# Replanned costs, a shared port that is counted fairly, and a weight-splitting step that may run on VectorE or ScalarE

## The chip, the cores and the metric

The kernel runs on one core of a Trainium2 chip. The metric is the device time of one execution in microseconds (us). The engines are TensorE (PE in the profile, PEld for its weight loads), VectorE (DVE), ScalarE (ACT), GpSimd (POOL) and SyncE (SP), which here issues all DMAs.

## What is computed

A chunked linear attention over 4 sequences of 768 tokens and 8 heads, and behind it two feed-forward layers of width 2048 on the 3072 tokens, with ELU and with Mish:

```python
# per chunk c of each sequence and head, cum = cumsum(log a):
M = einsum('bhin,bhjn->bhij', Cc, Bc) * exp(cum_i - cum_j) * causal
y = einsum('bhij,bhjd->bhid', M, xc) + einsum('bhin,bhnd->bhid', Cc, state) * exp(cum)
state = exp(sum(la)) * state + sum_j(Bc_j * xc_j * exp(cum_last - cum_j))
...
h = x @ w_in;  g = where(h > 0, h, exp(min(h, 0)) - 1);   x = g @ w_out      # layer 1
h = x @ w_in;  g = h * tanh(log1p(exp(min(h, 20))));      y = g @ w_out      # layer 2
```

The weights arrive in double precision, 64 bits each. Precision is kept by splitting each operand into a high and a low part and summing three products.

## The kernel before

The 3072 tokens go through the layers in seven blocks of 384, 384, 512, 512, 512, 512 and 256 columns, and each block of a layer in 16 slots, one for each 128 of the 2048 hidden units. A slot s is: six matmuls into a tile `h` (lines 769 to 771, `emit_h(s)`), the activation into `w` (ELU: `elu_1` on ScalarE line 785, `elu_2` on ScalarE line 791 or VectorE line 793, `elu_3` on VectorE lines 799 and 801; Mish: `mish_1`, ScalarE line 816), the split into `gh` (`split_hi`, lines 356 and 358) and `gl` (`split_lo`, line 812, GpSimd or VectorE), and the second product into `acc`. Slots 0 to 15 are layer 1 of block 0, 16 to 31 layer 1 of block 1, 32 to 47 layer 2 of block 0, and so on; h(s) stands below for the six matmuls of slot s. There are two `h` tiles in this phase, so h(s) waits until the activation has read h(s-2).

The attention runs in 32 tiles of 96 tokens, woven in between: a DMA brings the row `d`, `at_diff` adds to it (line 543, two halves, each on GpSimd or VectorE), `at_mask` masks it (GpSimd, line 547), `at_exp` takes the exponential (ScalarE, line 552), the scores are multiplied in (`at_p0`, line 654, or `at_p`, line 666, VectorE), and TensorE forms `ys` (line 697).

The weights come in 32 jobs of 256 by 256 double-precision numbers. A job has five steps. `job_1` takes the top three bits of each low word (VectorE, line 332, in place in the tile `raw`); `job_2` scales the high words (ScalarE, line 341, function Prelu); `job_3` joins both (VectorE, line 348); `job_4` makes the high part (line 356 on ScalarE or 358 on VectorE) and `job_5` the low part (line 372, GpSimd or VectorE).

Nothing in this order is written by hand. Every piece is a `step` with an engine (or several to choose from, `alt`), a cost in us, and its dependences. `run_steps` simulates the five engines by these costs: it takes the engine that can start soonest, on it the ready step with the least latest start `late`, and for a step with a choice the engine on which `end` is least. VectorE steps in the set `lock` are not started while a GpSimd step runs, nor the other way (`held`), since both use one port. ScalarE keeps one table of functions at a time: the planner charges LOAD, 1.4 us, for a switch between the tables of `exp` (also that of `job_2`) and of `mish`. What the plan gives is the order in which the instructions stand on each engine; on the chip each engine works through its own list and waits at the head of it.

Of the kernel before, what the change touches and what calls it, by code (L numbers as in the profile page):

```python
# [10 lines left out]
I32 = mybir.dt.int32  # L11
AF = mybir.ActivationFunctionType
# [5 lines left out]
def tile_chain(  # L18
# [54 lines left out]
    LOAD, HOLD = 1.4, 6.0  # L73

# [45 lines left out]
    def run_steps():  # L120
# [208 lines left out]
    def job_1(j):  # L329

        lw = raw[j][:, :, :, 0]
        nc.vector.tensor_scalar(  # L332
# [609 lines left out]
    for j, (key, k) in enumerate(jobs):  # L942
# [11 lines left out]
        q1 = step((V, 0.36, lambda j=j: job_1(j)), q0)  # L954
# [3 lines left out]
        q3 = step((V, 0.65, lambda j=j: job_3(j)), q1, q2)  # L958
# [28 lines left out]
    def out_of_y(i, y):  # L987

        YHI[i], YLO[i] = {}, {}
        for q in pieces(i):  # L990
            w = q[3] / T
            YHI[i][q[0]] = step((A, 0.11 + 0.1 * w, lambda q=q: at_y_hi(i, *q)), y, xy_f["x", q[0]][1])
            YLO[i][q[0]] = step((V, 0.07 + 0.2 * w, lambda q=q: at_y_lo(i, *q)), YHI[i][q[0]])
        return list(YHI[i].values()) + list(YLO[i].values())

    def three_parts(i, need):
# [3 lines left out]
        a1 = step((A, 0.82, lambda: at_split_1(i)), need, sn)  # L1000
        a2 = step(alt(lambda e: at_split_2(i, e), (V, 0.40), (G, 0.45)), a1, rn)
        a3 = step((A, 0.62, lambda: at_split_3(i)), a2)
        a4 = step(alt(lambda e: at_split_4(i, e), (V, 0.40), (G, 0.45)), a3)
# [7 lines left out]
    def two_scores(i, a5, tf, ex, r_n, cold):  # L1011
        pz = []
        for z in range(2):
            pf, pn = take("s")
            sc = step((PE, 0.4 if cold else 0.33, lambda z=z: at_scores(i, z)), a5, pn)
# [77 lines left out]
    for i in range(NB, tiles):  # L1093
# [26 lines left out]
        rc2 = step(alt(lambda e, i=i: at_rc2(i, e), (V, 0.27), (A, 0.41)), rc)  # L1120
# [33 lines left out]
    for s in range(len(order) * NF):  # L1154
# [11 lines left out]
        pe = 6 * (0.0115 + n / 2370)  # L1166
# [10 lines left out]
        ca, cv, ct, cg = 0.10 + n * 0.00071, 0.07 + n * 0.00052, 0.07 + n * 0.00104, 0.08 + n * 0.00243  # L1177
# [84 lines left out]
```

## Time and profile before

| | |
|---|---|
| median of three runs | 630.92 us (628.60 to 631.34) |
| the profiled execution | 628.61 us |
| its span, first to last instruction | 626.7 us |
| TensorE busy | 606.7 us (97%) |
| VectorE / ScalarE / GpSimd busy | 453.0 / 367.9 / 193.8 us |
| chain that ended last | PE 82%, DVE 10%, ACT 4%, issue 2% |

The span is shorter than the profiled execution by 1.9 us, which lie around it. TensorE's busy time includes the pipelined tails of matmuls, so its idle time, not its busy time, says where it waits. The chain that ended last is followed back from the last instruction: an engine with no share of it had its work hidden.

### The profile page before, as it was taken

The page shows a single profiled execution, that of the slowest core. Times are in us where ns is not written, and L with a number is a line of the kernel's source. Part 1 is how long each engine was busy: PE and PEld are TensorE (multiplying, and loading weights), DVE is VectorE, ACT ScalarE, POOL GpSimd, SP SyncE. Part 2 cuts the span into 40 slices and gives each one's busy share as a digit, 9 for nine tenths or more (in the row PEclk, how much of TensorE's full clock was granted, in tenths as well). Part 3 has the DMA queues.
Part 4 walks back from the last instruction along what each step waited for, and adds up shares of the span by engine and source line. Part 5 has one row for each costly group of instructions (what it writes and reads, how often), then busy time and mean ns, then how long its engine had stood idle before and what let it go on. Part 6 is the DMA issues. An engine that isn't in the chain of part 4 may idle for free.

```text
span 626.7 us, 10880 instructions
## 1 busy us (share of the span) xinstructions
PE 606.7 (97%) x3876; PEld 513.3 (82%) x3876; DVE 453.0 (72%) x885; ACT 367.9 (59%) x681; POOL 193.8 (31%) x243
## 2 busy tenths in 40 slices
PE   6899999899999999999999999999999999999996
PEld 5776789798988778888888888888888888988895
DVE  5989799998878888764768765878765445844453
ACT  4678887558776677543786645878644313542121
POOL 4456844255366466000454201435300000000000
PEclk9799999999999999999999999999999999999999
DMA  7889592013656545000545201444200001100010
GB/s 155 214 247 313 162 325 44 24 20 71 121 93 87 119 104 85 3 1 8 104 91 91 44 1 44 88 93 74 60 0 1 0 5 25 33 1 1 1 35 17
DMA packets 133653, 47.07 MB, mean 75 GB/s; under 512 B 116672, under 2 KB 122432, under 8 KB 133600
## 3 DMA queue, kind: packets, MB, share of 16 engines
q1 hardware_dynamic: 133600, 46.39, 33.1%
q8 instruction: 30, 0.49, 0.3%
q14 instruction: 23, 0.19, 0.1%
HBM read 32.31 MB, written 3.24 MB: 57 GB/s over the span
## 4 chain that ended last, share of the span: by engine, by line
PE 82%; DVE 10%; ACT 4%; issue 2%; DMA 1%; POOL 0%; DVEq 0%; ACTq 0%
PE acc L863 14%; PE h L769 13%; PE h L770 12%; PE h L771 12%; PE acc L864 7%; PE acc L832 5%; PE acc L833 5%; PE acc L834 5%; PE ys L697 2%; PE ys L727 2%; DVE raw L348 1%; PE s L660 1%; DVE raw L332 1%; PE acc L837 1%; DVE gl L812 1%
## 5 line engine op out<-in xcount | busy, mean ns | idle before, releaser
L769 PE MATMUL h<-xyh,wi 128*128 128x512 f32 (+2 forms) x448 | 167.2, 373 | 6.4 <-ACT w L816 3.7
L770 PE MATMUL h<-xyl,wi 128*128 128x512 f32 (+2 forms) x448 | 161.5, 361 | 0.0
L771 PE MATMUL h<-xyh,wi 128*128 128x512 f32 (+2 forms) x448 | 161.1, 360 | 0.0
L863 PE MATMUL acc<-wo,gh 128*128 128x512 f32 x384 | 142.3, 403 | 0.0
L812 DVE TENSOR_TENSOR gl<-w,gh 128x512 fp32r<-128x512 f32 (+2 forms) x187 | 124.2, 666 | 20.9 <-ACT gh L356 11.7
L816 ACT ACTIVATE w<-h 128x512 f32<-128x512 f32 (+2 forms) x112 | 59.5, 536 | 109.4 <-PE h L771 66.7
L864 PE MATMUL acc<-wo,gl 128*128 128x256 f32 x384 | 107.6, 280 | 0.0
L769 PEld LDWEIGHTS h<-xyh,wi 128*128 128x128 f32 x448 | 84.5, 189 | 23.1 <-ACT w L816 5.3
L358 DVE CAST gh<-w 128x512 fp32r<-128x512 f32 (+2 forms) x112 | 46.9, 420 | 69.2 <-PE acc L863 48.2
L771 PEld LDWEIGHTS h<-xyh,wi 128*128 128x128 f32 x448 | 84.5, 189 | 10.7
L770 PEld LDWEIGHTS h<-xyl,wi 128*128 128x128 f32 x448 | 84.7, 189 | 9.1 <-DVE xyl L714 0.5
L863 PEld LDWEIGHTS acc<-wo,gh 128*128 128x128 f32 x384 | 72.2, 188 | 15.4
L785 ACT ACTIVATE w<-h 128x512 f32<-128x512 f32 (+2 forms) x96 | 51.8, 542 | 52.5 <-PE h L771 35.0
L356 ACT ACTIVATE gh<-w 128x512 fp32r<-128x512 f32 (+2 forms) x96 | 55.3, 578 | 32.5 <-PE acc L833 23.3
L864 PEld LDWEIGHTS acc<-wo,gl 128*128 128x128 f32 x384 | 72.5, 189 | 1.7
L832 PE MATMUL acc<-gh,wo 128*128 128x512 f32 (+2 forms) x192 | 70.4, 366 | 0.9 <-DVE xyl L848 0.9
L812 POOL TENSOR_TENSOR gl<-w,gh 128x512 fp32r<-128x512 f32 (+2 forms) x21 | 26.1, 1242 | 142.0 <-ACT gh L356 112.5
L833 PE MATMUL acc<-gh,wo 128*128 128x512 f32 (+2 forms) x192 | 69.6, 363 | 0.0
L834 PE MATMUL acc<-gl,wo 128*128 128x512 f32 (+2 forms) x192 | 69.6, 363 | 0.0
L793 DVE TENSOR_SCALAR w<-w 128x512 f32<-128x512 f32 (+2 forms) x78 | 37.0, 476 | 36.5 <-ACT w L785 35.9
L801 DVE TENSOR_TENSOR w<-h,w 128x512 f32<-128x512 f32 (+2 forms) x78 | 48.8, 628 | 2.1
L543 POOL TENSOR_TENSOR d<-d,dk 96x384 f32<-96x384 f32 x36 | 34.4, 966 | 28.1 <-DMA d<-cum_d 20.5
(100 smaller groups left out, 848.4 us busy)
## 6 DMA issues: line engine op xcount, KB each, us to landing
d<-cum_d SPq DMA_DIRECT2D x31, 288.0 KB, 3.6
raw<-in_moe_w_in_dram SPq DMA_DIRECT2D x16, 512.0 KB, 6.0
raw<-in_moe_w_out_dram SPq DMA_DIRECT2D x16, 512.0 KB, 6.0
xs<-in_x_dram SPq DMA_DIRECT2D x32, 96.0 KB, 2.8
bc<-in_C_dram SPq DMA_DIRECT2D x32, 48.0 KB, 2.7
bc<-in_B_dram SPq DMA_DIRECT2D x32, 48.0 KB, 2.7
out_dram<-o SPq DMA_DIRECT2D x16, 96.0 KB, 1.9
bc<-bc SPq DMA_DIRECT2D x84, 16.0 KB, 1.9
```

The lines of the kernel that those rows point to most:

```text
L356: nc.scalar.activation(out=out, in_=in_, func=AF.Copy)
L769: nc.tensor.matmul(out=h, lhsT=hi[:, k, fs], rhs=xh[:, k, :], start=(k == 0), stop=False)
L770: nc.tensor.matmul(out=h, lhsT=hi[:, k, fs], rhs=xl[:, k, :], start=False, stop=False)
L771: nc.tensor.matmul(out=h, lhsT=lo[:, k, fs], rhs=xh[:, k, :], start=False, stop=(k == 1))
L785: nc.scalar.activation(out=new_w(s), in_=st[s][0], func=AF.Exp)
L812: alu(eng).tensor_tensor(out=gl, in0=w, in1=gh.bitcast(F32), op=ALU.subtract)
L816: nc.scalar.activation(out=new_w(s), in_=st[s][0], func=AF.Mish)
L832: nc.tensor.matmul(out=y, lhsT=hi[:, f % FP, ds], rhs=gh, start=(f == 0), stop=False)
L833: nc.tensor.matmul(out=y, lhsT=lo[:, f % FP, ds], rhs=gh, start=False, stop=False)
L834: nc.tensor.matmul(out=y, lhsT=hi[:, f % FP, ds], rhs=gl, start=False, stop=(f == NF - 1))
L863: nc.tensor.matmul(out=y, lhsT=gh[:, ts], rhs=w[:, :, f % FP, :], start=(f == 0), stop=False)
L864: nc.tensor.matmul(out=y[:, 0], lhsT=gl[:, ts], rhs=w[:, 0, f % FP, :], start=False, stop=(f == NF - 1))
```

## The change

All in the planner's numbers and rules, and one step with a second form:

- `job_1` may now run on ScalarE as well, there as a Copy of the low word, read as an unsigned integer, times 7.4999 / 2^32 and written as an integer; the planner chooses (VectorE 0.36, ScalarE 0.57). ScalarE gets 23 of the 32 jobs, VectorE keeps 9.
- In the comparison of engines (`end`), a choice between GpSimd and VectorE now counts the time for which the other one holds the port.
- A VectorE step that needs the port is held back when a GpSimd step that has no other engine is ready and more urgent by over YIELD, 2.0 us.
- Some twenty costs are new (below, a part of them).

```diff
-            r = max(free[e], ready(k, e))
+            r = max(free[e], ready(k, e), held[V] if e == G else held[G] if e == V and k in lock else 0.0)
...
+            wait_g = [(k, r) for k, o, r, _ in open_[G] if len(steps[k][0]) == 1 and free[G] <= free[V]]
...
                     if e == V and k in lock:
                         r = max(r, held[G])
+                        if any(late[q] + YIELD < late[k] and q2 <= max(r, free[V]) for q, q2 in wait_g if q != k):
+                            continue
...
-    def job_1(j):
+    def job_1(j, eng):
...
+        if eng == A:
+            nc.scalar.activation(out=lw, in_=lw.bitcast(U32), func=AF.Copy, scale=7.4999 * 2.0**-32)
+            return
...
-        q1 = step((V, 0.36, lambda j=j: job_1(j)), q0)
+        q1 = step(alt(lambda e, j=j: job_1(j, e), (V, 0.36), (A, 0.57)), q0)
...
-        q5 = step(alt(lambda e, j=j: job_5(j, e), (G, 1.33), (V, 0.60)), q4,
+        q5 = step(alt(lambda e, j=j: job_5(j, e), (G, 1.33), (V, 0.65)), q4,
...
-        a2 = step(alt(lambda e: at_split_2(i, e), (V, 0.40), (G, 0.45)), a1, rn)
+        a2 = step(alt(lambda e: at_split_2(i, e), (V, 0.50), (G, 0.50)), a1, rn)
...
-        ca, cv, ct, cg = 0.10 + n * 0.00071, 0.07 + n * 0.00052, 0.07 + n * 0.00104, 0.08 + n * 0.00243
+        ca, cv, ct, cg = 0.12 + n * 0.00080, 0.09 + n * 0.00058, 0.09 + n * 0.00110, 0.10 + n * 0.00243
```

Two places show what the new plan does to the lists of the engines.

VectorE at the start, from the first difference of tile 1 on (L543 is `at_diff`, L654 `at_p0`, L714 the low part of a tile's output), before:

```order
L543 TENSOR_TENSOR d<-d,dk 96x384
L654 TENSOR_TENSOR r<-s,d 96x192 x4
L543 TENSOR_TENSOR d<-d,dk 96x384
L358 COPY f32t<-p_tr 112x384
L654 TENSOR_TENSOR r<-s,d 96x192 x4
L543 TENSOR_TENSOR d<-d,dk 96x384
```

The same place of the changed kernel, whose lines are ten further down:

```order
L553 TENSOR_TENSOR d<-d,dk 96x384 x3
L664 TENSOR_TENSOR r<-s,d 96x192 x4
L553 TENSOR_TENSOR d<-d,dk 96x384 x2
L664 TENSOR_TENSOR r<-s,d 96x192 x4
L553 TENSOR_TENSOR d<-d,dk 96x384
L664 TENSOR_TENSOR r<-s,d 96x192 x4
```

All six differences of the tiles 1 to 3 now stand on VectorE, three of them ahead of the first `at_p0`; three stood on GpSimd.

ScalarE where the first Mish slots begin (L816 is `mish_1`, L356 the high parts `wi`, `wo` of weights and `gh`, L844 the high part of layer 1's result), before:

```order
L356 ACTIVATE wo_1433<-raw_1046 128x512
L816 ACT_TABLE_LOAD
L816 ACTIVATE w<-h 128x384
L356 ACTIVATE gh<-w 128x384
L356 ACTIVATE wi_1465<-raw_1061 128x512
L356 ACTIVATE wo_1491<-raw_1072 128x512
L816 ACTIVATE w<-h 128x384 x4
L844 ACTIVATE xyh<-acc 128x384
```

There in the changed kernel (L826 is `mish_1`, L340 `job_1` on ScalarE, L351 `job_2`, L534 a step of the attention):

```order
L826 ACT_TABLE_LOAD
L826 ACTIVATE w<-h 128x384 x2
L534 ACTIVATE stk<-r_1463 96x16x16
L534 ACTIVATE stk<-r_1465 96x8x32
L340 ACTIVATE raw_1178<-raw_1178 128x512
L351 ACT_TABLE_LOAD
L351 ACTIVATE raw_1178<-raw_1178 128x512
L826 ACT_TABLE_LOAD
L826 ACTIVATE w<-h 128x384 x2
L854 ACTIVATE xyh<-acc 128x384
```

The high parts of the weights that stood between the first two Mish steps have gone elsewhere, and a `job_2` now stands between Mish steps with a table load on both sides. Over slots 32 to 47 there was one such pair of loads (for an `at_exp`); there are five now, three for a `job_2` and two for an `at_exp`.

Counted by stages, in the order in which the plan issues its steps: between h(0) and h(48) VectorE has 29 `job_1` before and 7 now; ScalarE gets 10 between h(0) and h(16), 8 up to h(32) and 4 up to h(48). VectorE has there 5 `at_diff`, 4 `split_lo`, 2 `job_5` and 2 `job_4` more than before. After h(48) no `job_1` was left before, and none is now; VectorE has 4 `at_diff` and 4 `at_split_4` more there and 9 `split_lo` and 10 `elu_2` fewer.

## Rows read from the trace of the kernel before

**Rows 1.** Stretches from h(0), h(16), h(32), h(48) on: span, PE, PEld, DVE, ACT, POOL, PEclk.

```profile
0.00:23.00 23.00, 17.31 (x193) 14.32 (x193) 15.14 (x46) 11.61 (x23) 9.51 (x19) 0.81 0.76 167
23.00:71.30 48.30, 45.22 (x339) 34.30 (x337) 43.59 (x83) 39.32 (x78) 30.77 (x32) 0.99 0.94 269
71.30:108.40 37.10, 35.41 (x184) 32.07 (x183) 33.27 (x55) 28.16 (x59) 19.49 (x20) 1.00 0.56 162
108.40:148.70 40.30, 36.63 (x234) 33.39 (x233) 39.19 (x70) 24.46 (x46) 18.49 (x20) 1.00 0.13 25
148.70:621.30 472.60, 472.06 (x2936) 399.20 (x2934) 321.06 (x631) 263.86 (x479) 115.59 (x155) 1.00 0.26 49
```

**Rows 2.** TensorE in order of time: start, duration, instruction, in brackets the idle time before.

```profile
28.48 0.41 PE L769 MATMUL h<-xyh,wi 128*128 128x384 f32 x1 [1.45 <-ACT g L791]
39.28 0.92 PE L837 MATMUL acc<-g,raw 128*128 128x384 f32 x2 [0.81 <-DVE raw L348]
...
115.52 0.44 PE L769 MATMUL h<-xyh,wi 128*128 128x384 f32 x1 [1.73 <-ACT w L816]
119.39 0.45 PE L769 MATMUL h<-xyh,wi 128*128 128x384 f32 x1 [1.09 <-ACT w L816]
147.58 0.45 PE L769 MATMUL h<-xyh,wi 128*128 128x384 f32 x1 [0.85 <-ACT w L816]
```

**Rows 3.** Single lines: count, ns shortest/median/longest, first and last start, tile shapes.

```profile
L332 DVE TENSOR_SCALAR raw<-raw x32: 411/423/1249, 17.7 to 131.6; 128x512 int32<-128x512 int32 x32
...
L543 POOL TENSOR_TENSOR d<-d,dk x36: 827/840/1334, 10.3 to 437.6; 96x384 f32<-96x384 f32 x36
L543 DVE TENSOR_TENSOR d<-d,dk x26: 542/555/1665, 11.4 to 437.3; 96x384 f32<-96x384 f32 x26
```

**Rows 4.** The chain that ended last, between 72 and 120 us: start, duration, link.

```profile
75.49 1.13 ACT raw L341 x2
...
111.54 1.42 DVE raw L348
...
114.39 1.47 DVE raw L332 x2
```

**Rows 5.** ScalarE in order of time, around the first Mish slots; columns as in rows 2.

```profile
112.99 0.68 ACT L356 ACTIVATE wo<-raw 128x512 fp32r<-128x512 f32 x1 [1.51 <-DVE raw L348]
113.68 1.28 ACT L816 ACT_TABLE_LOAD   x1
114.97 0.49 ACT L816 ACTIVATE w<-h 128x384 f32<-128x384 f32 x1
...
118.30 0.67 ACT L356 ACTIVATE wo<-raw 128x512 fp32r<-128x512 f32 x1 [1.05 <-DVE wi L372]
118.87 0.47 ACT L816 ACTIVATE w<-h 128x384 f32<-128x384 f32 x1
```

**Rows 6.** ScalarE in order of time, the one pair of loads of slots 32 to 47.

```profile
143.59 1.28 ACT L552 ACT_TABLE_LOAD   x1
144.88 0.85 ACT L552 ACTIVATE d<-d 96x768 f32<-96x768 f32 x1
145.74 1.28 ACT L816 ACT_TABLE_LOAD   x1
147.04 0.49 ACT L816 ACTIVATE w<-h 128x384 f32<-128x384 f32 x1
```

**Rows 7.** VectorE, and one row of TensorE, in order of time at the start.

```profile
11.39 0.56 DVE L543 TENSOR_TENSOR d<-d,dk 96x384 f32<-96x384 f32 x1
11.98 1.15 DVE L654 TENSOR_TENSOR r<-s,d 96x192 f32<-96x192 f32 x4
13.05 1.13 DVE L543 TENSOR_TENSOR d<-d,dk 96x384 f32<-96x384 f32 x1
...
14.96 1.74 PE L648 MATMUL s<-f32t 16*96 16x96 f32 x16 [0.74 <-DVE r L654]
```

**Rows 8.** GpSimd's mask beside VectorE's `elu_2` and `elu_3`, in order of time.

```profile
25.73 1.21 POOL L547 TENSOR_SCALAR_AFFINE_SELECT d<-d 96x768 f32<-96x768 f32 x1 [0.55 <-DVE d L543]
...
26.12 1.03 DVE L793 TENSOR_SCALAR g<-g 128x384 f32<-128x384 f32 x1
...
27.78 0.56 DVE L801 TENSOR_TENSOR g<-h,g 128x384 f32<-128x384 f32 x1
```

More of the change, by code (lines that the diff above doesn't have):

```diff
@@ L11 @@
 I32 = mybir.dt.int32
+U32 = mybir.dt.uint32
 AF = mybir.ActivationFunctionType
@@ L73, in tile_chain @@
     LOAD, HOLD = 1.4, 6.0
+    YIELD = 2.0
     lock = set()
@@ L957, in tile_chain @@
         table[q2] = "exp"
-        q3 = step((V, 0.65, lambda j=j: job_3(j)), q1, q2)
+        q3 = step((V, 0.68, lambda j=j: job_3(j)), q1, q2)
         lock.add(q3)
         q4 = step(alt(lambda e, j=j: job_4(j, e), (A, 0.58), (V, 0.34)), q3, pn)
-        q5 = step(alt(lambda e, j=j: job_5(j, e), (G, 1.33), (V, 0.60)), q4,
+        q5 = step(alt(lambda e, j=j: job_5(j, e), (G, 1.33), (V, 0.65)), q4,
                   dl=slot_time(2 * NF + k * FP) + 10.0 if j >= NJ else 1e9)
@@ L991, in out_of_y @@
             w = q[3] / T
-            YHI[i][q[0]] = step((A, 0.11 + 0.1 * w, lambda q=q: at_y_hi(i, *q)), y, xy_f["x", q[0]][1])
-            YLO[i][q[0]] = step((V, 0.07 + 0.2 * w, lambda q=q: at_y_lo(i, *q)), YHI[i][q[0]])
+            YHI[i][q[0]] = step((A, 0.14 + 0.14 * w, lambda q=q: at_y_hi(i, *q)), y, xy_f["x", q[0]][1])
+            YLO[i][q[0]] = step((V, 0.10 + 0.2 * w, lambda q=q: at_y_lo(i, *q)), YHI[i][q[0]])
         return list(YHI[i].values()) + list(YLO[i].values())
@@ L999, in three_parts @@
         rf, rn = take("r1")
-        a1 = step((A, 0.82, lambda: at_split_1(i)), need, sn)
-        a2 = step(alt(lambda e: at_split_2(i, e), (V, 0.40), (G, 0.45)), a1, rn)
-        a3 = step((A, 0.62, lambda: at_split_3(i)), a2)
-        a4 = step(alt(lambda e: at_split_4(i, e), (V, 0.40), (G, 0.45)), a3)
+        a1 = step((A, 0.88, lambda: at_split_1(i)), need, sn)
+        a2 = step(alt(lambda e: at_split_2(i, e), (V, 0.50), (G, 0.50)), a1, rn)
+        a3 = step((A, 0.68, lambda: at_split_3(i)), a2)
+        a4 = step(alt(lambda e: at_split_4(i, e), (V, 0.50), (G, 0.50)), a3)
         tf, tn = take("t")
@@ L1014, in two_scores @@
             pf, pn = take("s")
-            sc = step((PE, 0.4 if cold else 0.33, lambda z=z: at_scores(i, z)), a5, pn)
+            sc = step((PE, 0.4 if cold else 0.38, lambda z=z: at_scores(i, z)), a5, pn)
             pz.append(step((V, 0.47, lambda z=z: at_p(i, z)), sc, ex, r_n))
@@ L1087, in tile_chain @@
         sp_ = step((PE, 0.19, lambda i=i: at_st(i)), bw, LX[i], an, SO.get(i - 1, []))
-        SO[i] = step((V, 0.34, lambda i=i: at_st_out(i)), sp_, LX[i + NB])
+        SO[i] = step((V, 0.41, lambda i=i: at_st_out(i)), sp_, LX[i + NB])
         bf.append(sp_)
@@ L1119, in tile_chain @@
         rc = step((V, 0.56, lambda i=i: at_rc(i)), cs, r_n)
-        rc2 = step(alt(lambda e, i=i: at_rc2(i, e), (V, 0.27), (A, 0.41)), rc)
+        rc2 = step(alt(lambda e, i=i: at_rc2(i, e), (V, 0.37), (A, 0.52)), rc)
         lock.add(rc2)
@@ L1142, in tile_chain @@
             y = step((PE, 0.76, lambda i=i: (at_y(i), at_st(i))), pz, rc, rc2, LX[i], pn, SO[i - NB], b1, b2)
-            SO[i] = step((V, 0.34, lambda i=i: at_st_out(i)), y, LX[i + NB])
+            SO[i] = step((V, 0.41, lambda i=i: at_st_out(i)), y, LX[i + NB])
             pf.append(SO[i])
@@ L1219, in tile_chain @@
             for k in range(NK[c]):
-                y = step((PE, 0.35, lambda s=s, k=k: emit_y2(s, k)), ydep, an[k] if an else [], YS[s][-1:], prev, dl=ydl)
+                y = step((PE, 0.347, lambda s=s, k=k: emit_y2(s, k)), ydep, an[k] if an else [], YS[s][-1:], prev, dl=ydl)
                 YS[s].append(y)
```

2 lines of the change are left out of this document (1 added, 1 removed).

## The prediction, made before the changed kernel ran

> **What bounds the kernel now.** I read the busy times by stages first, cut where the slots 0, 16, 32 and 48 begin [rows 1]. The last row there is the largest: from h(48) at 148.7 us to the last matmul TensorE is busy 472.06 of 472.60 us. Three quarters of the kernel are TensorE at work, and no order of the other engines can shorten them by more than the 0.54 us that it idles. What a new plan can win lies ahead of 148.7 us. There TensorE idles 3.08 us from h(0) to h(16) (48.30 - 45.22), 1.69 up to h(32) (37.10 - 35.41) and 3.67 up to h(48) (40.30 - 36.63): 8.44 us in all, 1.3% of the time. That is the ceiling, apart from the 23.0 us before h(0). The next thing to see in the same rows is who is full. VectorE is busy 43.59 of 48.30, 33.27 of 37.10 and 39.19 of 40.30 us; ScalarE 39.32, 28.16 and 24.46 us. So VectorE is the fullest engine beside TensorE (90, 90 and 97%), and ScalarE is not far behind in the first two stages (81 and 76%) and free in the third (61%).
>
> Then I read TensorE's own order of time for the waits [rows 2]. The five largest that I can tie to a cause are 1.45 us before h(2), 0.81 us before the first second product, and 1.73, 1.09 and 0.85 us between h(32) and h(48), all three behind a Mish step of ScalarE. Last the chain of waits [rows 4], which shows why ScalarE was late there: `job_1` and `job_3` of the weights on VectorE, 1.47 us for two `job_1` and 1.42 us for one `job_3`.
>
> Why these are so long: `job_1` takes 423 ns at the median and up to 1249, `at_diff` on VectorE 555 and up to 1665 [rows 3]. An `elu_2` took 1.03 us while GpSimd's mask ran from 25.73 to 26.94 us, and ended just behind it [rows 8]. VectorE's long cases are waits for the port.
>
> **The change part by part.** The sum is made against the profiled execution, 628.61 us (span 626.7 and 1.9 around it); it lies 2.31 us under the median of the runs, 630.92, and I carry the sum over to the median unchanged.
>
> *VectorE's load, h(0) to h(48).* It loses 22 `job_1`: 22 x 0.423 = 9.3 us [rows 3]. But the fair port hands work back: 5 differences, 4 `split_lo`, 2 `job_5` and 2 `job_4` more. At the 0.555 us of a difference for each, which is an estimate for the other eight, that is 13 x 0.555 = 7.2 us. Net -2.1 us of 125.7. GpSimd is relieved more: a difference that cost it 0.840 us holds the port for 0.555 on VectorE [rows 3]. So VectorE's stretched instructions get fewer, but its own list is hardly shorter.
>
> *ScalarE's load.* A `job_1` on ScalarE is not in the trace. The nearest row is `job_2`, of the same shape: two in a row took 1.13 us on the chain, 0.57 each [rows 4]; I take that, and 0.68, the single instruction's length in [rows 5] for this shape, as the upper end. By stages: 39.32 + 10 x 0.57 = 45.0 of 48.30 us (93%); 28.16 + 8 x 0.57 = 32.7 of 37.10 (88%). In the third stage come the loads of tables: five pairs in slots 32 to 47 instead of one. A load took 1.28 us and the next instruction began 0.01 us behind it [rows 6], so four more pairs cost 4 x 2.56 = 10.2 us: 24.46 + 4 x 0.57 + 10.2 = 37.0 of 40.30 (92%). ScalarE thus becomes as full as VectorE was. This is the reason why I don't book the ceiling.
>
> The Trainium skill, "ScalarE: Activation LUTs" (section "What ACT_TABLE_LOAD costs" and the rule on table sets behind it), speaks against this part of the change: it wants activations batched by table, and prices a switch at 1.28 us for the load and 1.38 us of draining, 2.66 us in all. By that, four more pairs would be 21.3 us and ScalarE would need 48.0 us of a stage of 40.3, some 8 us more than there are. The trace bears out the load and not the drain: the exponential began 0.01 us behind its load, so I give that outcome 0.02, within the slower cases below.
>
> *Before h(0).* Three differences now stand ahead of the first `at_p0` where one did [rows 7]: it can start at 11.39 + 3 x 0.56 = 13.07 instead of 11.98 us, 1.09 us later, and 0.9 us more if GpSimd's mask takes the port between them. Behind `at_p0` TensorE waits already (0.74 us at 14.96). Against that, the difference at 13.05 that took 1.13 us is gone from its place. I take +0.9 us, between 0 and +2.0.
>
> *h(2).* Its wait of 1.45 us ended with the `elu_2` and `elu_3` on VectorE at 26.12 and 27.78 [rows 2, 8]. `elu_2` of slot 0 goes to ScalarE, and a `job_5` between the two to GpSimd, while one more difference (0.555 us) comes ahead of them: the 1.03 us and the `job_5` go from the path, the difference joins it. I take -1.0, between -1.45 and 0.
>
> *The first second product* waited 0.81 us for a `job_3` [rows 2]. In the new order `job_1` of that job is on ScalarE, and its `job_3` stands ahead of slot 3's `elu_3`. I take -0.8, between -0.81 and 0: what is late next is the second product's own input, `elu_3`.
>
> *h(16) to h(32).* VectorE loses 7 `job_1` and ScalarE gains 8. Both end near 88%. I take 0, between -1.69 (all of TensorE's idle time) and +2.0, half of ScalarE's 4.6 us of new work shown, an estimate.
>
> *h(32) to h(48).* The waits of 1.73 and 1.09 us have one pattern: ScalarE stood 1.51 and 1.05 us at the head of its list for a weight step that VectorE had not fed yet, with the Mish step queued behind it [rows 5]. These two weight steps leave that place. But the load of the table at 113.68 stays, and two `job_1` and one `job_2` now stand before it. I book -1.0 of the first and all -1.09 of the second, about -2.1. The wait of 0.85 us stands behind the one pair of loads [rows 6]: from 143.59 to 147.04 ScalarE served no slot. Four more such pairs cost TensorE between 0 (from h(48) on pairs cost next to nothing: 0.54 us idle in all) and 4 x 0.85 = 3.4 us. I take 0.28 for each, a third of the row, since the two `h` tiles cover a part: +1.1. Net -1.0, between -3.67 and +3.4.
>
> *After h(48).* Between -0.5 and +1.0; 0.
>
> Sum: +0.9 - 1.0 - 0.8 + 0 - 1.0 + 0 = -1.9 us. 628.61 becomes 626.7, and the median 630.92 becomes **629.0 us**.
>
> **The rivals.** *The waits go (faster).* If the relieved port does what the stretched instructions suggest, VectorE gains its 2.1 us and a good part of the stretches: `job_1` alone stretched to 1249 ns against 423. Then most of TensorE's 8.44 us of idle time goes, say 7, and the start costs 0.9: -6.1, 624.8 us. For it speaks that all the named waits lead back to VectorE; against it that ScalarE, which feeds h(s), ends at 88 to 93%. It decides if the sum is under -3.15 us.
>
> *ScalarE becomes the bound (slower).* The place is slots 32 to 47: five times ScalarE serves no slot for about 3.4 us (two loads and what lies between, [rows 6]), and only two `h` tiles stand between it and TensorE. If each of the four new pairs shows 0.85 us, the first Mish load keeps its 1.73 us since ScalarE reaches it no sooner, and the start costs 0.9, the sum is +3.4 + 0.9 = +4.3 with nothing won at h(2) and the second product: 635.2 us. It decides from 0.56 us for each pair on, if nothing else is won (3.15 - 0.9 = 2.25, by 4).
>
> *It does not do what it says.* The plan is made of costs; if the real lengths differ (`job_1` on ScalarE 0.68 instead of 0.57: 22 x 0.11 = 2.4 us of ScalarE), the engines meet elsewhere than planned, one wait takes the place of another, and the time stays: 630.9 us, within the forecast's class.
>
> *TensorE's clock* is low in part of the first 23 us (granted 0.81 on the mean, [rows 1]) and full after. A later start could move that a little; I give it no term, and a share of the slower tail.
>
> **How the numbers follow.** A change of 0.5%, 3.15 us, is about what a measurement of this kernel can tell from none. Forecast and its neighbourhood, with the rival in which waits are exchanged: 0.42. Waits gone: 0.36. ScalarE the bound, or the start later than I think: 0.22. The range leaves out about one in ten at each end. It reaches down to nearly all lower ends together (-1.45 - 0.81 - 1.69 - 3.67 = -7.6 us) and up to nearly the slower rival's +4.3: 623.5 to 635.0 us.
>
> **What would show it.** Right: in the changed profile `job_1` on ScalarE at 0.57 to 0.68 us; ScalarE busy about 45, 33 and 37 us in the three stages; h(0) at about 24 us; no wait over 0.5 us before h(2) and the first second product; between h(32) and h(48) short waits behind the new loads; after h(48) the same 472 us. Wrong: a stage from h(48) on that is longer than before, which I have excluded by the idle time alone; ScalarE's busy time in the third stage under 30 us; or waits that vanish in the second stage, for which I have no named cause.

## The result, and the profile after

The changed kernel took 622.22 us at the median (619.80 to 622.84, four runs), the kernel before 631.12 us beside it (628.60 to 631.34, four runs). The ratio is 0.9866, 95% interval 0.9846 to 0.9886: 1.3% faster. The prediction of 629.0 us lay 6.8 us too high, the result 1.3 us under its range, and the likeliest class, no change, was wrong. The changed kernel once more, with no edit: 621.48 us, ratio 0.9881 (0.9852 to 0.9909). Put down before that run: if the difference between the medians (8.9 us) and the one between the two profiled executions (5.8) is chance, its profile lies 8 to 9 us under one of the kernel before, otherwise 6 again. Its profiled execution took 620.59 us, 8.0 us under the first profile of the kernel before; why that is the pair to compare is told in the part on the prediction.

The profiled execution of the changed kernel took 622.84 us (span 621.1). The first view is the stretches from h(0), h(16), h(32) and h(48) on, as in [rows 1]; columns: span, then busy time of PE, PEld, DVE, ACT, POOL, then PEclk, DMA share, GB/s.

```profile
0.00:25.30 25.30, 18.61 (x193) 14.71 (x193) 15.49 (x49) 12.56 (x25) 5.89 (x14) 0.84 0.77 174
25.30:70.80 45.50, 44.83 (x338) 34.37 (x337) 39.32 (x83) 41.57 (x83) 24.92 (x26) 0.98 0.90 255
70.80:106.00 35.20, 35.16 (x185) 32.14 (x184) 32.97 (x61) 34.62 (x72) 17.48 (x16) 1.00 0.68 195
106.00:142.10 36.10, 35.60 (x233) 33.50 (x233) 32.94 (x63) 32.09 (x51) 13.44 (x18) 1.00 0.16 29
142.10:615.80 473.70, 471.56 (x2936) 399.74 (x2934) 311.97 (x622) 263.38 (x484) 117.79 (x150) 1.00 0.26 48
```

Against [rows 1] the three stages ahead of h(48) are 2.8, 1.9 and 4.2 us shorter, 125.7 us down to 116.8 in all. TensorE idles 0.67, 0.04 and 0.50 us in them, 1.2 us instead of 8.4. The start is 2.3 us longer, and from h(48) on it is as before within 1.1 us. So the gain lies where the prediction looked for it, and it is nearly all of what was there.

The same interval in one row for each kernel, h(0) to h(48), before, after and the changed kernel once more:

```profile
23.00:148.70 125.70, 117.26 (x752) 99.77 (x751) 116.05 (x207) 91.93 (x181) 68.75 (x71) 0.99 0.57 159
...
25.30:142.10 116.80, 115.59 (x751) 100.02 (x751) 105.23 (x205) 108.27 (x204) 55.85 (x59) 0.99 0.61 167
...
24.00:140.80 116.80, 116.10 (x752) 100.75 (x752) 104.57 (x205) 108.44 (x204) 56.14 (x59) 0.98 0.62 167
```

VectorE has 205 instructions there instead of 207, but they take 105.23 instead of 116.05 us: 513 ns on the mean, not 561. It lost short steps and got longer ones (differences for `job_1`), and still became 10.8 us faster, because its instructions wait less for the port: GpSimd is busy 55.85 instead of 68.75 us. Two kinds of step show it, `job_3` and `split_lo` between h(0) and h(48), first before, then after (count, busy us, mean ns, idle time before):

```profile
L348 DVE SCALAR_TENSOR_TENSOR raw<-raw 128x512 int32<-128x512 int32 x30 | 25.2, 849 | 0.0
L812 DVE TENSOR_TENSOR gl<-w,gh 128x384 fp32r<-128x384 f32 x19 | 15.7, 828 | 0.8 <-ACT gh L356 0.6
```

```profile
L358 DVE SCALAR_TENSOR_TENSOR raw<-raw 128x512 int32<-128x512 int32 x30 | 23.0, 772 | 0.7 <-ACT raw L340 0.6
L822 DVE TENSOR_TENSOR gl<-w,gh 128x384 fp32r<-128x384 f32 x24 | 15.1, 641 | 0.6 <-ACT gh L366 0.4
```

Added up over the whole list, with overlaps between neighbours counted twice, the durations are 128.9 us before and 116.7 after. At the shortest that the traces of all runs show for each kind of instruction and shape, the two lists would take the same, 102.4 and 102.3 us. What is beyond that is 26.5 us before and 14.4 after, and 25.7 and 13.2 us of it lie in instructions that overlap one of GpSimd. So VectorE's gain is length, not the number of its steps. ScalarE is 16.3 us fuller and no stage shows it.

TensorE's waits over the whole span (what waited, for whom, us in total, times, longest):

```profile
...
PE s L670 <- DMA t<-stk: 1.6, 1, 1.6
PE s L658 <- DVE r L664: 1.1, 2, 0.9
PE ys L707 <- PE s L658: 1.0, 1, 1.0
PE h L779 <- DVE g L809: 0.7, 1, 0.7
...
```

Of the five waits of [rows 2] none is left: before h(2), before the first second product, and the three behind Mish steps. A wait of 0.7 us (at 34.0 us, before h(4)) and one of 0.4 take their place ahead of h(48). Of the lines shown, the two in the middle are ahead of h(0), the first is new and behind h(48). The chain that ended last says the same in one line (it was PE 82%, DVE 10%, ACT 4%):

```profile
PE 92%; DMA 3%; issue 2%; DVE 2%; SPq 0%; ACT 0%; POOL 0%; POOLq 0%; DVEq 0%
```

The moved step, on ScalarE and on VectorE (count, ns shortest/median/longest, first and last start, forms), and ScalarE in order of time around one `job_2` that now stands between Mish steps:

```profile
L340 ACT ACTIVATE raw<-raw x23: 649/671/740, 22.0 to 119.9; 128x512 int32<-128x512 uint32 x23
...
L342 DVE TENSOR_SCALAR raw<-raw x9: 416/420/1515, 19.3 to 121.6; 128x512 int32<-128x512 int32 x9
```

```profile
111.30 0.67 ACT L340 ACTIVATE raw<-raw 128x512 int32<-128x512 uint32 x1
111.98 1.28 ACT L351 ACT_TABLE_LOAD   x1
113.28 0.69 ACT L351 ACTIVATE raw<-raw 128x512 f32<-128x512 f32 x1
113.98 1.28 ACT L826 ACT_TABLE_LOAD   x1
115.27 0.87 ACT L826 ACTIVATE w<-h 128x384 f32<-128x384 f32 x2
```

`job_1` costs ScalarE 671 ns as a single instruction and 0.57 us from its start to that of the next, at the median; I had taken 0.57. Behind the pair of loads the next two Mish steps come together (x2). No wait of TensorE for ScalarE stands there: from 111.19 to 115.95 us it has the `h` matmuls and the second products of two slots each to do, and the 0.4 us that it waits next are for VectorE.

### The profile page after: what moved, and what is told of

Read it like the earlier page. It is cut to its first block, busy times and chain, and to the rows that moved or that the text cites. A ratio compares the mean times of both kernels' runs of the same rounds, so it can differ in the third digit from the quotient of the medians.

```text
span 621.1 us, 10932 instructions
## 1 busy us (share of the span) xinstructions
PE 605.8 (98%) x3876; PEld 514.5 (83%) x3876; DVE 433.4 (70%) x877; ACT 384.7 (62%) x712; POOL 179.5 (29%) x222
## 4 chain that ended last, share of the span: by engine, by line
PE 92%; DMA 3%; issue 2%; DVE 2%; SPq 0%; ACT 0%; POOL 0%; POOLq 0%; DVEq 0%
PE acc L873 15%; PE h L779 14%; PE h L780 14%; PE h L781 14%; PE acc L874 7%; PE acc L842 6%; PE acc L843 6%; PE acc L844 6%; PE acc L847 3%; PE ys L707 2%; PE ys L737 2%; PE s L670 1%; DMA t<-stk 1%; PE s L658 1%; DMA raw<-in_moe_w_out_dram 1%
## 5 line engine op out<-in xcount | busy, mean ns | idle before, releaser
L822 DVE TENSOR_TENSOR gl<-w,gh 128x512 fp32r<-128x512 f32 (+2 forms) x182 | 120.7, 665 | 26.4 <-ACT gh L366 17.5
L826 ACT ACTIVATE w<-h 128x512 f32<-128x512 f32 (+2 forms) x112 | 58.9, 536 | 100.8 <-PE h L781 66.3
L779 PEld LDWEIGHTS h<-xyh,wi 128*128 128x128 f32 x448 | 84.6, 189 | 15.8 <-DVE g L809 1.0
L366 ACT ACTIVATE gh<-w 128x512 fp32r<-128x512 f32 (+2 forms) x98 | 57.4, 586 | 30.0 <-PE acc L843 24.6
L822 POOL TENSOR_TENSOR gl<-w,gh 128x512 fp32r<-128x512 f32 (+2 forms) x26 | 29.5, 1136 | 152.1 <-ACT gh L366 119.2
L844 PE MATMUL acc<-gl,wo 128*128 128x512 f32 (+2 forms) x192 | 69.6, 362 | 0.0
L803 DVE TENSOR_SCALAR w<-w 128x512 f32<-128x512 f32 (+2 forms) x69 | 28.4, 412 | 25.7 <-ACT w L795 24.6
L811 DVE TENSOR_TENSOR w<-h,w 128x512 f32<-128x512 f32 (+2 forms) x69 | 43.4, 629 | 1.7
L842 PEld LDWEIGHTS acc<-gh,wo 128*128 128x128 f32 x192 | 36.2, 188 | 5.4 <-DVE xyl L858 0.4
```

What stands on the lines that cost most here:

```text
L366: nc.scalar.activation(out=out, in_=in_, func=AF.Copy)
L779: nc.tensor.matmul(out=h, lhsT=hi[:, k, fs], rhs=xh[:, k, :], start=(k == 0), stop=False)
L822: alu(eng).tensor_tensor(out=gl, in0=w, in1=gh.bitcast(F32), op=ALU.subtract)
L826: nc.scalar.activation(out=new_w(s), in_=st[s][0], func=AF.Mish)
L842: nc.tensor.matmul(out=y, lhsT=hi[:, f % FP, ds], rhs=gh, start=(f == 0), stop=False)
L844: nc.tensor.matmul(out=y, lhsT=hi[:, f % FP, ds], rhs=gl, start=False, stop=(f == NF - 1))
```

## The experiments

All ratios are to the kernel before, run beside the experiment. "h(0) to h(48)" is from the profiled execution.

### One half of the change at a time: the move and the order

The first kernel keeps the old order and sends the same 23 `job_1` to ScalarE at the places where they stood:

```diff
+KEEP = (0, 2, 4, 8, 10, 12, 16, 19, 31)
...
+        if j not in KEEP:
+            nc.scalar.activation(out=lw, in_=lw.bitcast(U32), func=AF.Copy, scale=7.4999 * 2.0**-32)
+            return
```

> The order of the kernel before, untouched; only the 23 job_1 that the new plan gives to ScalarE are issued there, at the same places of the program. Theory A (VectorE's list was the bound, and job_1 off it is the gain): most of the gain without a new plan, 625 us or less. Theory B (the gain is in the new order, which fits the weight steps between the slots): 630 to 633 us, since ScalarE's list, in an order that was not made for it, holds up the activations.

Measured: 626.90 us, 0.9967 (0.9953 to 0.9982), between what the two theories ask.

The second kernel has the changed kernel's order, with all 32 `job_1` issued on VectorE:

```diff
-        q1 = step(alt(lambda e, j=j: job_1(j, e), (V, 0.36), (A, 0.57)), q0)
+        q1 = step(alt(lambda e, j=j: job_1(j, V), (V, 0.36), (A, 0.57)), q0)
```

> The order of the changed kernel, untouched; only all 32 job_1 are issued on VectorE, at the same places of the program. Theory A: VectorE gets 22 x 0.42 = 9.3 us back ahead of h(48) and most of the gain is lost, 628 us or more. Theory B: the order keeps most of the gain, 625 us or less.

Measured: 630.78 us, 1.0018 (0.9996 to 1.0040), as Theory A expects. h(0) to h(48) of both:

```profile
24.20:147.50 123.30, 118.66 (x753) 101.71 (x752) 103.27 (x186) 102.27 (x202) 65.22 (x71) 0.97 0.57 160
...
25.30:152.50 127.20, 121.06 (x752) 104.96 (x752) 119.19 (x228) 97.85 (x183) 59.54 (x59) 0.95 0.56 154
```

The move alone gives a quarter of the gain, although VectorE is then as little busy (103.27 us) as in the changed kernel; the order alone gives nothing, with VectorE at 119.19 us. The profile of the first is the longest of its ten executions (628.46 us); it still waits 1.9 us behind two Mish steps and 1.3 us for the reader of `acc` (`xyl`). In the profile of the second, also the longest of its ten, 10.4 us at half of the clock add to the waits (last section). So VectorE's lower load is not the gain by itself: the step has to leave VectorE, and the lists have to be drawn up for that.

### One part of the planner's change at a time

Four kernels were planned anew. Without the two rules for the port:

```diff
-            r = max(free[e], ready(k, e), held[V] if e == G else held[G] if e == V and k in lock else 0.0)
+            r = max(free[e], ready(k, e))
...
-                        if any(late[q] + YIELD < late[k] and q2 <= max(r, free[V]) for q, q2 in wait_g if q != k):
-                            continue
```

> The changed kernel, planned without the two rules on the port (the held time in the choice between GpSimd and VectorE, and YIELD); choice for job_1 and new costs stay. If these rules carry a part of the gain: 624 us or more. If the choice for job_1 with a plan made for it carries it: 621 to 623 us.

Measured: 623.74 us, 0.9919 (0.9895 to 0.9943), between the two cases. With the rules and the new costs, but no choice for `job_1`:

```diff
-        q1 = step(alt(lambda e, j=j: job_1(j, e), (V, 0.36), (A, 0.57)), q0)
+        q1 = step((V, 0.36, lambda j=j: job_1(j, V)), q0)
```

> The changed kernel, planned anew without the choice for job_1, which is VectorE's alone as before; port rules and new costs stay. If new costs and rules are worth something by themselves: 625 to 627 us. If they only pay with job_1 off VectorE: 628 to 631 us, as the kernel before.

Measured: 626.89 us, 0.9960 (0.9941 to 0.9978), the first case: they are worth something by themselves. The kernel before with the choice and nothing else:

```diff
-        q1 = step((V, 0.36, lambda j=j: job_1(j)), q0)
+        q1 = step(alt(lambda e, j=j: job_1(j, e), (V, 0.36), (A, 0.57)), q0)
```

> The kernel before, planned anew with the choice for job_1 alone; old costs, old rules. If the gain is the relief of VectorE by job_1 in an order made for it: 621 to 624 us, nearly all of the gain. If the new costs and rules are needed for it: 626 to 629 us, like the move without a new order (626.9).

Measured: 622.61 us, 0.9891 (0.9875 to 0.9908), the first case: nearly all of the gain. And the changed kernel with all old costs (choice and rules stay):

> The changed kernel replanned with all old costs; the choice for job_1 and both rules for the shared port stay. It parts the new costs from the rules. So far: the choice alone with a plan made for it 0.9891 of the kernel before, everything 0.987 to 0.988, everything but the rules 0.9919. Theory A (the choice with any plan made for it is the gain, the rest is exchange of one wait for another): 0.986 to 0.992. Theory B (the rules need the new, longer costs, since held times are made of costs): the old costs under the new rules leave waits, 0.994 or more.

Measured: 621.58 us, 0.9885 (0.9870 to 0.9900), as Theory A expects. h(0) to h(48) of the four, in this order:

```profile
23.60:144.60 121.00, 116.85 (x777) 101.04 (x776) 109.17 (x202) 100.40 (x202) 62.37 (x68) 0.99 0.67 171
...
25.50:146.50 121.00, 116.53 (x744) 100.32 (x743) 112.48 (x216) 88.01 (x174) 53.32 (x57) 0.99 0.59 161
...
23.50:144.40 120.90, 117.41 (x756) 100.64 (x755) 112.16 (x199) 100.82 (x196) 68.28 (x69) 0.99 0.62 167
...
23.90:142.00 118.10, 117.04 (x753) 100.70 (x752) 102.54 (x201) 105.16 (x204) 56.26 (x59) 0.98 0.62 166
```

The choice alone, with a plan made for it, holds 1.1 of the 1.2 to 1.3%; the rules and costs alone 0.4%. In these profiles each half takes 4.7 or 4.8 of the 8.9 us between h(0) and h(48), and both together take all of them, by two ways: the choice cuts the number of VectorE's instructions (199 for 207), the rules cut their length (112.48 us for 216). But the kernel without the choice has eight matmuls of scores ahead of its h(0) that stood behind it. Counted from VectorE's copy `dec` at 11 to 12 us, ahead of which executions of one kernel differ, the way to h(48) is 132.9, 134.9, 132.8 and 130.9 us in the four, 137.6 before and 129.7 in the changed kernel. By that, the rules and costs alone take 2.8 of 7.9 us and the choice alone 4.8. In the medians the second half adds less to the first: 0.9891 and 0.9866 to 0.9881 have intervals that overlap, while 0.9919, without the rules, lies 0.4 to 0.5% above. So what the rules add to the choice is not settled: between nothing and 0.5%. The new costs add nothing that shows.

### Two costs that the prediction had feared

Nine differences put back on GpSimd, in the changed kernel's order, and, in another kernel, `job_2` of the jobs 29 to 31 as a Copy (which changes their negative weights), so that three of the five pairs of table loads in slots 32 to 47 go:

```diff
+BACK = ((1, 1), (2, 1), (3, 1), (4, 1), (5, 0), (5, 1), (6, 0), (7, 0), (8, 0))
...
+        if (i, h0 // 4) in BACK:
+            eng = G
```

```diff
+        if j >= 29:
+            nc.scalar.activation(out=hw, in_=hw, func=AF.Copy, scale=2.0**-111)
+            return
```

> The order of the changed kernel; only the nine halves of at_diff ahead of h(48) that stood on GpSimd before and stand on VectorE now go back to GpSimd, at the same places (three of them in the first 23 us). If the fair port in the choice of engines matters: VectorE's own list is shorter by 9 x 0.55 = 5.0 us but GpSimd holds the port 7.6 us more, and the time rises by 2 us or more, to 624 to 627 us. If it does not matter, or if VectorE's own list is the bound: 622 us or less; the start alone could win 1 us.

> The changed kernel; only the job_2 of the jobs 29, 30 and 31 is a Copy instead of Prelu, so three of the five pairs of table loads in the first Mish slots are gone (negative weights of these three jobs are not turned as they should be; same shapes and counts). If a pair of loads that stands between Mish steps shows on TensorE, as I had booked at 0.28 us each and up to 0.85: 1 to 3 us faster than the changed kernel, 619 to 620.5. If the two h tiles and the planned place cover them wholly: the same, 621.5.

Measured: 620.56 us, 0.9874 (0.9841 to 0.9908), and 621.81 us, 0.9876 (0.9859 to 0.9892). h(0) to h(48):

```profile
23.30:140.10 116.80, 116.30 (x752) 100.90 (x751) 104.56 (x199) 108.27 (x204) 62.15 (x65) 0.98 0.62 171
...
24.20:140.80 116.60, 116.10 (x751) 100.77 (x751) 104.57 (x205) 100.83 (x198) 56.19 (x59) 0.98 0.61 169
```

Neither moves the time, as the second case of each had it. With six differences fewer in this stretch VectorE is busy as long as with them (104.56 against 104.57 us): what it does not do itself it waits for at the port. ScalarE without three pairs of loads is 7.6 us less busy and TensorE is not faster. These three pairs cost nothing here; the two for an `at_exp` were not removed.

### How much reserve the two engines have

ScalarE was busy 91, 98 and 89% of the three stages, and no wait showed it. So its work was raised on purpose, by a second Copy behind each of its 23 `job_1`, over the whole tile and, in another kernel, over half of it (values unchanged):

```diff
+            nc.scalar.activation(out=lw, in_=lw.bitcast(U32), func=AF.Copy, scale=1.0)
```

```diff
+            l0 = raw[j][:, 0, :, 0]
+            nc.scalar.activation(out=l0, in_=l0.bitcast(U32), func=AF.Copy, scale=1.0)
```

> The changed kernel with a second Copy of the same shape (128x512, scale 1) behind each of the 23 job_1 on ScalarE; the order is otherwise the same, and the values stay what they were. At the 0.57 us from start to start that the changed kernel's trace shows for two ACTIVATEs of this shape in a row, ScalarE gets 22 x 0.57 = 12.5 us more ahead of h(48): 5.7, 4.6 and 2.3 us in its three stages, of which it is 91, 98 and 89% busy. Theory A (ScalarE's busy share counts, the reason for which the prediction did not book the whole idle time): the second stage has 0.6 us of ScalarE's time left, so most of its 4.6 us show, and 1.7 us of the 5.7 in the first stage: together +5 to +6 us, 627 us, ratio to the kernel before about 0.995. Theory B (ScalarE's work is ahead of need and only the two h tiles' activations count): each second Copy delays at most the one activation behind it, covered by the h tiles; under +2 us, ratio 0.986 to 0.990.

> The changed kernel with a second Copy over half the tile (128x256) behind each of the 23 job_1 on ScalarE. An ACTIVATE of 128x256 takes about 0.33 us from start to start (an estimate from 0.57 us for 128x512 and 0.49 us for one of 128x384 in the trace of before), so ScalarE gets 22 x 0.33 = 7 us more ahead of h(48), half of the run with whole second Copies, which cost 9.7 us of time for 12.5 us of work. Theory A (ScalarE has no slack in the new plan; each us of its work shows at about 0.8): +5.5 us, 627 us, ratio 0.997 to the kernel before. Theory B (there is a reserve of about 3 us, the difference of 12.5 and 9.7, and behind it everything shows): +4 us, 625.5 us, 0.995. Theory C (the reserve is larger and the loss grows faster than the dose): under +3 us, 624.5 us or less.

And VectorE got back what the change had taken from it, one TENSOR_SCALAR of the old `job_1`'s shape ahead of each of these jobs' `job_3`, in the new order and with ScalarE's 23 left where they are:

```diff
+        if j in on_act:
+            nc.vector.tensor_scalar(
+                out=lw, in0=lw, scalar1=0, scalar2=7, op0=ALU.logical_shift_right, op1=ALU.bitwise_and
+            )
```

> The changed kernel with one more instruction on VectorE ahead of each of the 23 job_3 whose job_1 is on ScalarE, of the kind and shape of the old job_1 (128x512, shift by 0 and the lowest three bits, values unchanged, 0.42 us). VectorE thus has the 22 x 0.42 = 9.3 us back that the change took from it ahead of h(48), in the new order, while ScalarE keeps its 22 job_1. Theory A (VectorE's time was the limit, and its relief is the gain): the waits ahead of h(48) come back, +5 us or more, 627 us or more, ratio 0.997 or more. Theory B (the new order is the gain, and VectorE's list has reserve where job_3 stands): under +2 us, 624 us or less, ratio 0.992 or less.

Measured: 631.19 us, 1.0042 (1.0028 to 1.0056); 626.02 us, 0.9943 (0.9925 to 0.9961); 634.05 us, 1.0073 (1.0049 to 1.0096). h(0) to h(48), in this order:

```profile
24.10:151.10 127.00, 119.83 (x751) 101.09 (x751) 106.29 (x205) 121.42 (x226) 57.13 (x59) 0.98 0.57 156
...
24.00:145.70 121.70, 117.93 (x751) 100.91 (x751) 105.20 (x205) 116.32 (x226) 56.95 (x59) 0.98 0.58 160
...
24.60:154.80 130.20, 121.29 (x752) 103.93 (x752) 122.86 (x228) 108.76 (x205) 57.63 (x59) 0.96 0.56 150
```

*ScalarE.* The doses are larger than expected, because the second Copy reads what the first wrote and begins 0.71 us behind its start instead of 0.57. By starts the whole Copy adds 0.71 + 0.58 - 0.57 = 0.72 us, 22 times 15.8 us; the half 0.71 + 0.35 - 0.57 = 0.49 us, 10.8 us. Against 621.5 us the times rose by 9.7 and 4.5 us (by the ratios, 10.1 and 3.9). Both leave the same remainder: 15.8 - 9.7 = 6.1 and 10.8 - 4.5 = 6.3 us. By ScalarE's busy time, which rose by less, 13.2 and 8.0 us, the remainders are 3.5 and 3.5. So ScalarE had a reserve of some 3.5 to 6 us ahead of h(48), of the 8.5 us that it idles there (116.8 - 108.3), and behind it each us showed (5.2 us of time for 5.0 us of work between the two doses). The whole dose cost more than Theory A had asked (9.7 us for 5 to 6). Theory B of the half dose, a reserve and then a straight cost, holds; its reserve of 3 us is the one by busy time, by starts it is twice as large.

*VectorE.* 22 x 0.42 = 9.2 us of work came back and the time rose by 12.5 us, past the kernel before. Theory A holds, by more than its 5 us: VectorE had no reserve that shows, and the work stretched its neighbours: its busy time rose from 105 to 122.86 us, by 17.6 us for 9.2. A part of the 12.5 us is TensorE's clock, 3.4 us at its lower level behind each of the two longest waits (last section). The place of the longest wait, first VectorE's list, then GpSimd's, then TensorE's (start, duration, instruction, in brackets the idle time before), and last VectorE's list at the same place of the changed kernel:

```profile
86.23 0.42 DVE L362 TENSOR_SCALAR raw<-raw 128x512 int32<-128x512 int32 x1
86.68 1.39 DVE L365 SCALAR_TENSOR_TENSOR raw<-raw 128x512 int32<-128x512 int32 x1
...
88.46 1.75 DVE L547 TENSOR_TENSOR stk<-r,stk 96x128 bf16<-96x128 f32 x2
90.14 1.01 DVE L865 SCALAR_TENSOR_TENSOR xyl<-acc,xyh 128x384 fp32r<-128x384 f32 x2
```

```profile
86.31 1.21 POOL L829 TENSOR_TENSOR gl<-w,gh 128x384 fp32r<-128x384 f32 x1 [0.81 <-ACT gh L373]
87.48 1.74 POOL L389 TENSOR_TENSOR wo<-raw,wo 128x512 fp32r<-128x512 f32 x1
```

```profile
90.74 0.69 PE L849 MATMUL acc<-gh,wo 128*128 128x384 f32 x1 [3.02 <-DVE xyl L865]
91.22 0.52 PE L850 MATMUL acc<-gh,wo 128*128 128x384 f32 x1
```

```profile
82.09 2.46 DVE L540 TENSOR_TENSOR stk<-r,stk 96x128 bf16<-96x128 f32 x2
84.47 1.01 DVE L858 SCALAR_TENSOR_TENSOR xyl<-acc,xyh 128x384 fp32r<-128x384 f32 x2
```

The added step takes 0.42 us; the `job_3` behind it 1.39 us where its median is 0.69, beside GpSimd's 1.21 us. The two pieces of the attention are stretched in both kernels, to 1.75 us here and to 2.46 in the changed one, where two at their median of 0.28 us would take 0.57. So it is not this place alone that makes the wait: VectorE comes to it late. The reader of `acc` (`xyl`), which frees the accumulator for TensorE, begins 18.0 us behind h(16) (72.1 us) here and 13.7 us behind it (70.8 us) in the changed kernel. TensorE stands still for 3.02 us; in the changed kernel it goes on there without such a gap.

### Why the kernel before is slower than its first profile

Its profiled execution (628.61 us) lay 2.5 us under its median, the changed kernel's 0.6 us over its own. Most of the 2.5 us lies in that median of four runs: beside the experiments the kernel before had medians of 628.64 to 629.74 us, over 8 to 19 runs each. Two more profiles were taken of it, with no edit:

> The kernel before once more, for another profiled execution. Its first profile lies 2.5 us under its median. Theory A: other executions have TensorE waits that last longer than the ones of the first profile, by landing times of DMAs, and a stretch of lower granted clock behind one of them, as the kernels in the old order (job_1 moved) and with the new order alone showed (3.4 and 6.8 us at about half of the clock, 1.7 to 3.4 us each): span 628 to 631 us with such a stretch. Theory B: the executions differ evenly, in the start and the end: the same waits, no stretch of lower clock behind h(0), span 626 to 628 us.

> The kernel before a third time, for a further profiled execution, with the same two theories: with a stretch of lower granted clock behind a TensorE wait ahead of h(48) the span is 628 to 631 us; without one 626 to 628 us.

Measured: 629.52 us (span 627.5) and 630.63 us (span 628.7). h(0) came at 23.5 and 24.2 us, where the first profile has 23.0. And both have what the first has not, a stretch of low granted clock behind a TensorE wait ahead of h(48). First the one of the third profile, then that of the second, then the place in the first profile that has the same wait as the second (1.73 and 1.74 us) and no such stretch:

```profile
55.00:57.70 2.70, 1.69 (x13) 1.25 (x13) 2.67 (x5) 1.45 (x3) 2.28 (x3) 1.00 1.04 337
57.70:61.10 3.40, 3.40 (x10) 2.37 (x8) 3.37 (x8) 2.77 (x6) 0.94 (x1) 0.50 1.03 367
61.10:70.00 8.90, 8.90 (x73) 6.66 (x72) 7.37 (x15) 7.42 (x15) 6.38 (x6) 1.00 0.96 301
```

```profile
114.00:117.60 3.60, 1.86 (x14) 1.49 (x13) 3.59 (x7) 2.90 (x5) 1.41 (x1) 1.00 0.00 0
117.60:121.10 3.50, 3.46 (x18) 2.96 (x16) 3.50 (x9) 1.80 (x4) 0.00 (x0) 0.51 0.00 0
```

```profile
113.00:117.00 4.00, 2.27 (x19) 1.90 (x18) 4.00 (x8) 3.30 (x5) 1.41 (x1) 1.00 0.00 0
117.00:120.50 3.50, 2.41 (x17) 2.00 (x14) 3.50 (x9) 1.75 (x4) 0.00 (x0) 1.00 0.05 17
```

From h(0) to the last matmul the three profiles take 598.1, 598.5 and 598.9 us. So of the 2.0 us between the first and the third, 1.2 come ahead of h(0) and 0.8 behind it. Theory A is right that the stretches are there, but not about their price or about longer waits (from h(0) to h(48) TensorE idles 7.3 us in the second profile and 8.4 in the first, and the second's span of 627.5 us lies under the 628 asked). The larger part of the difference is the start, which Theory B had named. Why a stretch costs so little shows in the second profile: the slower matmuls fill the next wait. From the `h` behind the wait to the `h` of the next slot it takes 3.92 us (116.29 to 120.21), and 3.87 us in the first profile (115.52 to 119.39), where the clock was full and TensorE waited 1.09 us more in between.

## Why the prediction was wrong

The sum was -1.9 us. Between profiles that agree in their first 11 us (628.61 and 620.59 us, see "From the profile to the median") the change is -8.0 us: the start +1.0 (booked +0.9), up to h(16) -2.6 (-1.8), up to h(32) -2.2 (0), up to h(48) -4.1 (-1.0), behind it -0.1 (0). Nearly all that is missing was left out of the two stages from h(16) to h(48), and two readings led to that.

**The load of VectorE, the step that failed.** I counted its list: 22 `job_1` fewer, 13 other steps more, net -2.1 us, and concluded that it was hardly shorter. The list is: 205 instructions for 207 (seven steps net that the count did not name came to it as well, among them four `r<-bc,stk` of 0.28 us). What I did not put into the sum is their length, though I had read it: [rows 3] and [rows 8] show the stretched ones, and I called them waits for the port. Work taken off GpSimd (68.75 down to 55.85 us busy) takes stretches off VectorE, and its busy time fell by 10.8 us, five times what I booked. I gave that to the rival in which the waits go, at 0.36, instead of to a term. The restored `job_1` shows the same relation the other way: 9.2 us of work, 17.6 us of busy time. The load is a condition of the gain and not the whole of it: with the move in the old order VectorE was as little busy, and a quarter was won.

**ScalarE as the reason to leave the ceiling unbooked, which failed as well.** The forecast of its load was fair (45, 33 and 37 us forecast; 41.6, 34.6 and 32.1 measured), its reading was not. I took 93, 88 and 92% as a sign that waits would stay. Measured at 91, 98 and 89%, TensorE idles 1.2 us in all and no wait among them is for ScalarE, and the dose runs give it 3.5 to 6 us of reserve. A busy share next to one says that an engine has little reserve, not that anybody waits for it.

**h(16) to h(32).** Booked 0, since "both end near 88%" (measured: VectorE 94%, ScalarE 98%); measured -1.9, all of the stage's idle time. This is the sign of error that I had named (waits that vanish in the second stage).

**h(32) to h(48).** Booked -1.0, measured -4.2. The two Mish waits went wholly, as the mechanism said (-2.8 for the -2.1 booked); the 0.85 us behind the old pair of loads went too, and the four new pairs, booked at +1.1, show no cost: without three of the five the time is the same. The two `h` tiles cover such a pause of ScalarE in the rows above, where it serves two Mish steps ahead of it and two together behind it. The Trainium skill, "ScalarE: Activation LUTs" (section "What ACT_TABLE_LOAD costs"), prices a switch at 1.28 us for the load and 1.38 us of draining. Here too the load is 1.28 us, but it begins 0.01 us behind the instruction ahead of it (111.98) and the next begins 0.02 us behind it (113.28), so that the trace agrees with the first half only.

**h(2) and the first second product.** Booked -1.8, measured -2.8 for the stage. Right in kind.

**The idle time as a ceiling.** TensorE's idle time ahead of h(48) was 8.44 us, and I called it the ceiling. The stretch became 8.9 us shorter, since TensorE's busy time fell as well (117.26 to 115.59 us in the first pair of profiles): ends of matmuls are modelled, and part of a wait can lie in a busy time; that this is the cause is not shown.

**The start.** Booked +0.9. Measured +2.3 in the first pair of profiles, +1.0 in the second profile of the changed kernel. The kernel before has h(0) at 23.0, 23.5 and 24.2 us in its three profiles, the changed one at 25.3 and 24.0. What differs between executions lies ahead of VectorE's copy `dec`, which waits for TensorE: it starts at 11.07, 11.55 and 12.26 us before, at 12.37 and 11.10 in the changed kernel. From there to h(0) it is 11.9 us in all three profiles before and 12.9 in both of the changed kernel. So the change costs 1.0 us, as booked. The cause shows in VectorE's list, where the first `at_p0` now stands behind three differences instead of one [rows 7]; with three of the differences of the start back on GpSimd (and six later ones) the way is 12.3 us, so these account for 0.6 of the 1.0. The copy before, and the list of the changed kernel:

```profile
11.07 0.30 DVE L358 COPY dec<-p_d 32x128 f32<-32x128 f32 x1 [1.69 <-PE p_d L483]
```

```profile
12.37 0.30 DVE L368 COPY dec<-p_d 32x128 f32<-32x128 f32 x1 [2.76 <-PE p_d L493]
12.69 1.49 DVE L553 TENSOR_TENSOR d<-d,dk 96x384 f32<-96x384 f32 x3
14.22 1.15 DVE L664 TENSOR_TENSOR r<-s,d 96x192 f32<-96x192 f32 x4
```

**After h(48).** Booked 0; +1.1 with one new wait of 1.6 us for a transfer (`t<-stk`), 472.5 us in the second profile. Right.

**From the profile to the median.** Profile against profile the change is -5.8 us (628.61 to 622.84), close to the -6.1 of the rival in which the waits go; the medians differ by 8.9. I carried the sum over unchanged. That pair sets a kernel with an early `dec` (11.07 us) against one with a late one (12.37). Pairs that agree in `dec` differ by 8.0 us (628.61 and 620.59, `dec` at 11.07 and 11.10) and 7.8 us (630.63 and 622.84, at 12.26 and 12.37). The change is thus about -8 us, more than the -6.1 of that rival, and to carry it over unchanged cost the forecast 1 us at most. That the stretches of low clock behind waits make the kernel before longer or more uneven in its other executions is not shown: no other execution of it was profiled.

**TensorE's clock.** I called it full after the first 23 us; [rows 1] have 0.99 up to h(16). The low stretch of the start ends 1.4 us behind h(0) there and 1.9 and 3.8 us behind it in the two profiles of the changed kernel. I had given it no term, and none shows: up to h(16) these two take 45.5 and 45.7 us.

What stays open: what the port rules add to the choice (between nothing and 0.5%), and when a wait of TensorE is followed by low clock and when not.

## What to carry to other kernels

Where two engines share a port, cost a change by what it takes off either of them, and count the stretched instructions of the other as part of the gain: here the number of instructions stayed and their time fell by a tenth. Read a busy share as reserve, not as waiting, and measure the reserve with a dose of harmless work on that engine, two doses if it matters: what does not show is the reserve. Move a step and plan again; one without the other gave a quarter and nothing. And before two profiles are compared, find the first row in which they part: here 1.3 us of their difference lay ahead of `dec`, where executions of one kernel differ as much.

## What the runs showed of the hardware

**TensorE's clock behind short waits.** Each profile has a low stretch at the start that ends 1.4 to 4.6 us behind h(0). After it the granted clock is full in 11 of the 16 profiles; in the other five it stood at its lower level, 1.2 GHz for 2.4, for 3.4 us behind some waits: behind 1.0 us idle in the third profile of the kernel before and 1.74 us in the second (above), behind 1.34 us with the moved `job_1` in the old order, behind 3.02 and 2.3 us with `job_1` restored on VectorE. With the new order and all `job_1` on VectorE it was 7.0 us in one place and 3.4 us in another:

```profile
80.00:88.70 8.70, 6.84 (x33) 5.50 (x31) 8.41 (x13) 7.46 (x17) 5.75 (x6) 1.00 0.31 104
88.70:95.70 7.00, 6.19 (x20) 6.04 (x20) 6.56 (x16) 3.33 (x8) 2.24 (x3) 0.51 0.75 209
```

Behind 1.73 us in the first profile of the kernel before and 1.54 us with ScalarE's work doubled it stayed full, so the length of the wait alone doesn't decide. Where it is low, matmuls of this shape follow each other at 0.32 us instead of 0.17 (91.22, 91.55, 91.86 us in the run with `job_1` restored). A wait of TensorE can thus be followed by slower matmuls, in one execution and not in the next; in the kernel before they cost little, since they ran where it would have waited again.

**An instruction that reads what the one ahead of it on ScalarE wrote** began 0.71 us behind that one's start, where an independent one began 0.57 us behind it (128x512, medians): 0.14 us for the dependence.
